# A new order of the same units, with eight products on another engine

## The chip, the cores and the metric

The kernel runs on one core of a Trainium2 chip. A core has five engines that work side by side, each on its own queue of instructions: TensorE (PE) multiplies matrices from SBUF into PSUM, and its weight loads (PEld) are a stream beside the matmuls; VectorE (DVE) and ScalarE (ACT) work element by element and read PSUM as well as SBUF; GpSimd (POOL) works element by element on SBUF; SyncE (SP) issues all the transfers of this kernel. Engines wait for each other through semaphores. The metric is the device time of one execution in microseconds (us); less is better.

## The reference

Two independent parts share S = 2048 positions and D = 576 channels, and their results stand side by side in the output.

```python
# part A: a short convolution, a gate, a long convolution, a gate
for t in range(ks):                                   # ks = 4
    k_shift = k_shift + k_pad[:, t:t + S, :] * shift_k[:, ks - 1 - t][None, None, :]
kv = k_shift * v
y = irfft2(rfft2(kv_pad) * rfft2(kf_pad))[:, 0, :S, :]    # length 2*S
a = q * (y + kv * ssm_D)
# part B: linear attention, 32 heads of 18
q, k, v = split(x @ wqkv)
phi = lambda t: jnp.where(t > 0, t + 1, jnp.exp(t)) + 1e-6
kv = einsum("bhsd,bhse->bhde", phi(k), v);  z = einsum("bhsd->bhd", phi(k))
o = einsum("bhqd,bhde->bhqe", phi(q), kv) / (einsum("bhqd,bhd->bhq", phi(q), z)[..., None] + 1e-6)
b = o.reshape(B, S, D) @ wo
```

All data is bf16. `ssm_k` has one filter of 2048 taps for each channel.

## The kernel before

The work is cut into 333 units, each a small function. `ORDER` is a text that names every unit once, in the order in which they are emitted; each engine gets its instructions in that order and runs them in that order. After the `@` of a unit stand the PSUM banks that it uses (eight banks of 512 f32), and letters before it say which engine copies the result out of PSUM: A for ACT, D for DVE. So the order of `ORDER` sets, on every engine and on SP's queue, who stands behind whom; semaphores do the rest.

Part A takes the 576 channels in five chunks (128, 128, 64, 128, 128). `h` is the filter, `u` the gated input. For each chunk: `hl` loads the filter, `hd` adds ssm_D to its first tap (ACT), `hT` transposes it on PE. `cv` is the short convolution, in four stages: a product of k with the broadcast weights Wj into `at` (L495, L497), a sum (L498), and at the end the gate with v (L501). The long convolution is a Fourier transform in two steps: `h1`, `u1` multiply with the tables G (L530), and their results Ch and Cu are transposed by DMA (`ht`, `ut`, L538) into Cth and Ctu, `h2`, `u2` multiply with a small table W (L554) into T and SU. `pX` and `pT` are the products of the two spectra (L565, L567). `i1` and `j1` are the first step back (L580, with V as the result), `i2` the second, with the tables F, and the gate with q (L601, L602, L608). `sv` and `st` store. The tables G come from `ix` (the index, L146 to L153) and `sin` (L218); the second table takes the absolute value of the index, `mc`, computed on DVE (L153).

Part B: `q`, `kt` and `k` are the projections (L477, L471, L453, L462), each followed by phi: an exponential on ACT (L447) and a minimum and maximum on DVE (L448) that reads the result in SBUF and the projection in PSUM. `Gt` and `G` multiply phi(k) with x (L651, L663); `kv`, `M`, `z`, `ez`, `den`, `bc` are the small matrices and the normalisation (`bc` is L744 and L750 for the wide part, L755 and L758 for the rest); `o` and `ot` the output (L771, L774, L785, L788), stored by `os`.

At the start `wu` issues 40 matmuls on zeros (L80) that wait for one memset of DVE. `wm` writes a row of ones and zeros into the weights wq and wk (L366, L367), so that the bias-like extra row of x is handled by the same matmul; `lw` loads wq and wk. `xl` loads x, `xT` and `xU` transpose two of its four parts on PE and `xd` two by DMA. POOL makes index tables and masks (`hc`: L89 to L115) and clears rows. `fz` and `wx` are places for filler matmuls; with the letter N they emit nothing.

Two helpers matter. `evict` (L298 to L302) copies PSUM to SBUF on ACT or DVE. `in_turn` (L396) is called in front of a product: where it runs on POOL, DVE first clears one element and POOL copies that element, so that POOL's product can't begin before DVE has come to this place in its own queue. In the kernel before no unit has the letter P, so nothing of this is emitted.

Of the kernel before, what the change touches and what calls it, by code (L numbers as in the profile page):

```python
# [27 lines left out]


ORDER = """  # L30
wm hl.0 io wu.0 wx.5.N@0 wx.3.N@1 wx.2.N@2 wu.40@3 ix.0 hd.0 iw wx.1.N@0 sin.1 xl.1 wk id wx.4.N@0 ix.1 hT.0.A@4
xU.1.D@0 xT.1.D@6 ls Wj.0.A@2 wx.0.N@0 Wj.1.A@0 xl.3 one h1.0.0.1.D@4 iv xU.3.D@6 xT.3.D@2 h1.0.1.1.D@0 sin.0 sw
W lw.0 q.1.0@4 q.1.4@5 q.1.2@6 lw.1 kt.1@2 k.6@0 k.4@1 eps k.7@3 kl.0 cv.0.0. q.3.4@2 cv.0.1. h1.0.0.0.A@4
kt.3@0 hl.1 cv.0.2. h1.0.1.0.A@6 hd.1 k.5@1 q.1.1@3 q.1.3@2 q.3.3@4 q.3.2@0 hT.1.A@6 vl.0 hl.2 k.13@5 k.14@1
k.15@2 hd.2 q.3.0@3 cv.0.3. ht.0.0 h2.0.0.0.A@6 h2.0.0.1.A@4 k.12@0 q.3.1@1 hc h1.1.1.1.A@2 xd.2 q.2.4@4 k.9@5
h1.1.1.0.A@6 k.8@2 kt.2@0 cv.1.0. cv.1.1. hl.4 hd.4 h1.1.0.0.A@6 k.11@1 h1.1.0.1.A@4 ht.0.1 fz.7.N@0
h2.0.1.0.A@2 h2.0.1.1.A@6 q.2.1@0 q.2.3@4 k.10@2 cv.1.2. u1.0.1.0.A@6 xd.0 k.3@1 q.0.4@0 u1.0.0.0.A@4 kt.0@2
q.0.0@3 xl.2 u1.0.1.1.A@6 k.0@4 cv.1.3. u1.0.0.1.A@0 q.0.3@2 ht.1.0 h2.1.0.1.A@6 h2.1.0.0.A@4 k.1@0 cv.2.0. xl.0
k.2@1 ht.1.1 h2.1.1.0.A@6 h2.1.1.1.A@4 cv.2.1. cv.2.2. FT.0 Gt@3 u1.1.0.0.A@6 fz.4.N@0 u1.1.0.1.A@4 fz.6.N@0
u1.1.1.1.A@0 q.0.1@2 cv.2.3. G.4@6 ut.0.0 u2.0.0.0.A@4 ut.0.1 u2.0.1.0.D@0 q.2.0@2 u1.2.0.1.A@6 fz.3.N@3  # L40
u1.1.1.0.A@4 z@3 hT.2.D@0 u2.0.1.1.A@6 ez@2 den.3@3 den.1@4 u2.0.0.1.A@0 Wj.2.A@2 pX.0.0. pT.0.0. u1.2.1.0.A@6
FT.1 G.3@5 kl.1 u1.2.0.0.A@0 bc.1.0@26 q.0.2@4 u1.2.1.1.A@0 q.2.2@5 ut.1.1 u2.1.1.1.A@2 u2.1.1.0.A@6 ut.1.0
pX.0.1. ut.2.0 h1.2.1.1.A@0 ql.0 G.2@4 h1.2.1.0.A@2 hl.3 vl.1 pT.0.1. cv.3.0. cv.3.1. i1.0.1@60 den.0@5
j1.0.1.AA@60 h1.2.0.0.A@2 G.0@4 u2.1.0.1.A@6 i1.0.0@02 pX.1.1. pT.1.1. u2.1.0.0.A@4 j1.0.0.AA@02 cv.3.2. G.1@6
pX.1.0. pT.1.0. bc.0.0@40 h1.2.0.1.A@2 lwv hd.3 i2.0.0.A@6 i2.0.1.A@2 hT.3.A@4 cv.3.3. ht.2.0 i1.1.1@60
j1.1.1.AA@60 h1.3.0.1.A@2 kv@4 h1.3.0.0.A@6 h1.3.1.0.D@0 h1.3.1.1.A@2 u2.2.0.0.A@4 u2.2.0.1.D@6 h2.2.0.0.D@0
h2.2.0.1.A@2 den.2@4 lwo M.4@6 M.2@2 M.3@0 pX.2.0. i1.1.0@64 bc.1.4@2 bc.2.4@0 j1.1.0.AD@64 M.1@2 bc.0.4@0
ht.3.0 h2.3.0.1.D@6 pT.2.0. h2.3.0.0.A@4 i2.1.1.A@2 M.0@0 ht.3.1 u1.3.1.0.A@6 u1.3.0.1.D@4 u1.3.1.1.A@2 hT.4.D@0
u1.3.0.0.A@6 ut.3.1 cv.4.0. i2.1.0.A@4 h2.3.1.0.A@2 i1.2.0@06 h2.3.1.1.A@4 cv.4.1. cv.4.2. j1.2.0.AA@06 o.0.AA@2
ot.0.A@4 i2.2.0.A@0 i2.2.1.A@6 fz.9.F@2 u2.3.1.0.A@4 bc.2.0@20 h1.4.0.0.A@6 h1.4.1.1.A@4 h1.4.1.0.A@2  # L50
h1.4.0.1.A@6 u2.3.1.1.A@0 ot.2.A@4 fz.8.N@2 cv.4.3. o.2.DA@2 ut.3.0 u2.3.0.0.A@6 u2.3.0.1.D@0 pX.3.0. st
ot.1.A@4 u1.4.1.1.A@2 ht.4.1 pT.3.0. ht.4.0 u1.4.0.1.A@6 u1.4.0.0.A@4 os.0 o.3.DA@0 u1.4.1.0.A@2 os.7 i1.3.0@64
os.6 h2.4.1.0.A@0 pX.3.1. j1.3.0.AA@64 os.2 h2.4.1.1.D@2 pT.3.1. ut.4.0 o.1.AD@0 h2.4.0.1.D@2 h2.4.0.0.A@6
i1.3.1@40 bc.3.4@6 j1.3.1.AA@40 bc.3.0@26 ut.4.1 ql.1 u2.4.0.0.A@4 u2.4.0.1.A@2 pX.4.0. os.5 o.4.AD@0 pT.4.0.
fz.0.N@2 ot.3.A@4 o.5.DA@6 os.4 os.9 u2.4.1.1.A@2 i1.4.0@40 u2.4.1.0.D@6 pX.4.1. os.8 pT.4.1. j1.4.0.AA@40
o.6.AA@2 os.12 os.1 os.3 os.14 i2.3.1@6 sv.3.1 os.10 i2.3.0@4 sv.3.0 fz.2.N@0 i1.4.1@02 j1.4.1.DA@02 o.7.DA@6
os.15 os.13 os.11 i2.4.0@4 sv.4.0 i2.4.1@2 sv.4.1 fz.5.N@0 fz.1.F@0
"""


# [78 lines left out]
def _dft_index(tc, slot, K, part):  # L139

    nc = tc.nc
    if part == 0:
# [4 lines left out]

        nc.vector.tensor_scalar(out=K.mp[:], in0=K.mp[:], scalar1=19, scalar2=19, op0=ALU.logical_shift_left,
                                op1=ALU.arith_shift_right)
# [91 lines left out]
def kernel(  # L241
# [121 lines left out]
    def one_w():  # L363

        for w in (wk, wq):
            nc.vector.memset(w[0:64, 4, :].bitcast(I32), 0)  # L366
# [519 lines left out]
```

## Time and profile before

| what | value |
|---|---|
| time, median of 3 runs | 173.18 us (170.98 to 174.4) |
| time of the profiled execution | 170.53 us |
| its span, first to last instruction | 168.8 us |
| granted TensorE clock, mean | 0.99 |
| busiest engine | PE, 91% of the span |
| data moved | 31.83 MB, mean 189 GB/s |

The profile of an execution lists how long each engine was busy, cuts the span into slices, groups instructions by their line in the kernel (L530 is line 530), and says for each idle stretch which other instruction ended it ("<-"). "issue" is time in which an engine waited for nothing that the profile shows. x16 behind a group is the number of its instructions. SPq is SP's queue; for a transfer, its row there is the time that SP took to issue it, and "to landing" the time from issue until the data is there. Busy times of PE are modelled from pipelined matmuls and overlap.

### The profile page before, as it was taken

How to read it: one execution, taken by the hardware profiler on the slowest of the kernel's cores; microseconds unless marked ns; L12 is line 12 of the kernel's file. 1: busy time of each engine (PE TensorE's matmuls, PEld its weight loads, DVE VectorE, ACT ScalarE, POOL GpSimd, SP SyncE). 2: the span in 40 equal slices, each digit the busy share in tenths (PEclk: the TensorE clock that was granted, in tenths of full speed). 3: DMA queues.
4: the chain of work that ended last, by engine and by line, in shares of the span. 5: the costliest groups of instructions: out<-in, count | busy, mean ns of one | idle time of the engine just before them, and what ended most of it. 6: DMA issues, size and time to landing. Idle time of an engine off the chain costs nothing.

```text
span 168.8 us, 6523 instructions
## 1 busy us (share of the span) xinstructions
PE 153.5 (91%) x2899; PEld 96.9 (57%) x2920; DVE 146.8 (87%) x183; ACT 130.7 (77%) x172; POOL 22.3 (13%) x57
## 2 busy tenths in 40 slices
...
GB/s 131 293 317 267 337 252 155 233 161 203 152 220 193 179 140 132 267 184 53 204 346 260 82 215 156 128 128 6 123 147 296 159 196 169 165 276 83 201 240 91
DMA packets 74464, 31.83 MB, mean 189 GB/s; under 512 B 52361, under 2 KB 73859, under 8 KB 74436
## 3 DMA queue, kind: packets, MB, share of 16 engines
...
q8 instruction: 22, 0.36, 0.9%
...
HBM read 14.90 MB, written 4.72 MB: 116 GB/s over the span
## 4 chain that ended last, share of the span: by engine, by line
PE 75%; DVE 9%; ACT 8%; issue 3%; DVEq 1%
PE banks L663 10%; PE banks L530 9%; PE banks L453 9%; PE banks L477 8%; PE banks L771 7%; PE banks L580 5%; PE banks L554 5%; ACT V L300 3%; PE banks L517 3%; PE banks L80 3%; ACT T L300 2%; PE banks L601 2%; PE banks L602 2%; DVE at L498 2%; PE banks L651 2%
## 5 line engine op out<-in xcount | busy, mean ns | idle before, releaser
L300 ACT ACTIVATE V<-banks 128x1024 bf16<-128x1024 f32 (+1 forms) x22 | 21.4, 1026 | 5.6 <-PE banks L580 5.0
L530 PEld LDWEIGHTS <-G 128*128 128x128 bf16 x320 | 17.8, 98 | 5.8 <-issue 2.5
L453 PE MATMUL banks<-wk,xT 128*128 128x512 bf16 x73 | 18.7, 379 | 0.5 <-issue 0.2
L477 PE MATMUL banks<-xT,wq 128*128 128x512 bf16 x77 | 18.8, 380 | 0.2
L300 ACT ACTIVATE Cu<-banks 128x1024 bf16<-128x1024 f32 (+1 forms) x19 | 17.0, 940 | 1.2 <-ACT T L300 1.0
L498 DVE TENSOR_TENSOR at<-at 128x2048 bf16<-128x2048 bf16 (+1 forms) x15 | 17.5, 1164 | 0.5
L663 PE MATMUL banks<-pk,x_sb 128*128 128x512 bf16 (+1 forms) x77 | 17.6, 379 | 0.2
L497 DVE TENSOR_TENSOR at<-k,Wj 128x2048 bf16<-128x2048 bf16 (+1 forms) x15 | 17.0, 1131 | 0.1
L300 ACT ACTIVATE Ch<-banks 128x1024 bf16<-128x1024 f32 (+1 forms) x17 | 15.2, 928 | 1.3 <-PE banks L530 1.1
L771 PE MATMUL banks<-late_w,pqT 128*128 128x512 bf16 x57 | 14.8, 380 | 0.6 <-ACT T L300 0.2
L300 ACT ACTIVATE SU<-banks 128x1024 bf16<-128x1024 f32 x14 | 14.2, 1029 | 0.6 <-PE banks L554 0.5
L300 ACT ACTIVATE T<-banks 128x1024 bf16<-128x1024 f32 x14 | 13.9, 1039 | 0.2 <-PE banks L554 0.2
L448 DVE SCALAR_TENSOR_TENSOR pk<-pk,banks 128x512 bf16<-128x512 bf16 (+1 forms) x20 | 12.3, 630 | 1.5 <-ACT pk L447 1.4
L447 ACT ACTIVATE pk<-banks,neg 128x512 bf16<-128x512 f32 (+1 forms) x20 | 12.6, 656 | 1.2 <-PE banks L453 1.1
L447 ACT ACTIVATE pqT<-banks,neg 128x512 bf16<-128x512 f32 x16 | 11.0, 693 | 2.6 <-PE banks L477 2.2
L663 PEld LDWEIGHTS <-x_sb 128*128 128x128 bf16 (+1 forms) x80 | 7.7, 100 | 8.4
L580 PE MATMUL banks<-W,X 32*128 32x64 bf16 x576 | 11.2, 190 | 1.4 <-issue 1.4
L565 DVE TENSOR_TENSOR X<-SU,T 128x2048 bf16<-128x2048 bf16 x9 | 10.8, 1202 | 1.8 <-ACT SU L300 1.2
L530 PE MATMUL banks<-hT,G 128*128 128x128 bf16 (+1 forms) x160 | 11.1, 214 | 1.2 <-ACT Ch L300 0.9
L453 PEld LDWEIGHTS <-xT 128*128 128x128 bf16 x80 | 7.2, 98 | 8.5 <-issue 1.6
L477 PEld LDWEIGHTS <-wq 128*128 128x128 bf16 x80 | 7.2, 98 | 8.4 <-issue 1.0
L448 DVE SCALAR_TENSOR_TENSOR pqT<-pqT,banks 128x512 bf16<-128x512 bf16 x16 | 10.6, 682 | 1.5 <-ACT pqT L447 1.4
(146 smaller groups left out, 312.9 us busy)
## 6 DMA issues: line engine op xcount, KB each, us to landing
...
```

The lines of the kernel that those rows point to most:

```text
L300: nc.scalar.activation(out=out, in_=in_, func=ACT.Copy)
L447: nc.scalar.activation(out=out_ap, in_=ps_ap, func=ACT.Exp, bias=K.neg1[0:n, :])
L448: nc.vector.scalar_tensor_tensor(out=out_ap, in0=out_ap, scalar=1.0, in1=ps_ap, op0=ALU.min, op1=ALU.max)
L453: nc.tensor.matmul(ps, lhsT=xT[r // 4][:, t, r % 4 * 128:(r % 4 + 1) * 128], rhs=wk[:, t, 0:512], start=(t == 0), stop=(t == 4))
L477: nc.tensor.matmul(ps, lhsT=wq[:, t, 128 * c:128 * c + 128], rhs=xT[g][:, t, :], start=(t == 0), stop=(t == 4))
L497: in_turn(on[0]).tensor_tensor(out=t_, in0=kk[:, 3 - stage:19 - stage], in1=wb(stage), op=ALU.mult)
L498: in_turn(on[1]).tensor_tensor(out=a_, in0=a_, in1=t_, op=ALU.add)
L530: nc.tensor.matmul(ps[:, bi, 0:dc].rearrange("p (z h y) -> p z h y", z=2, y=8), lhsT=K.G[ri][:, b, :], rhs=xf(b).rearrange("p (h z y) -> p ...
L565: in_turn(on).tensor_tensor(out=s['X', hf][:], in0=s['SU', hf][:], in1=t[:, :, ::-1, :], op=ALU.mult)
L580: nc.tensor.matmul(ps[r][:, j, z, g, :], lhsT=s[key, hf][q:q + 32, z, x, 128 * g:128 * g + 128], rhs=K.W[q:q + 32, m, :], start=(n == 0), ...
L663: nc.tensor.matmul(ps[0:fn, :], lhsT=x_sb[:, r, f0:f0 + fn], rhs=pk[:, r, 0:512], start=(r == 0), stop=(r == 15))
L771: nc.tensor.matmul(ps[:, hh, :], lhsT=pqT[:, 4 * g + 2 * hh + i, c, :], rhs=B['M'][:, c, 0:512], start=(c == 0), stop=False)
```

## The change

`ORDER` is replaced by another order of the same 333 units, with other banks and other letters for the copies. Eight products now carry the letter P and run on POOL: the sum of stage 2 and the first product of chunk 1 in the short convolution (`cv.0.2.DP`, `cv.1.0.P`), and of the spectra `pX.1.0`, `pT.2.0`, `pX.3.1`, `pT.3.0`, `pT.4.1`, `pT.4.0`. The rows of `wm` are written by POOL, and the absolute value of the index is taken by ACT. The remaining lines of the kernel stay; all line numbers after `ORDER` grow by one. At the start of SP's queue the order of loads was h, x, shift weights, x, wq, wk, k, h; it becomes h, shift weights, x, x, h, wq, wk, k, and three transposes of Ch now follow before the first DMA transpose of x, where it was one.

```diff
 ORDER = """
-wm hl.0 io wu.0 wx.5.N@0 wx.3.N@1 wx.2.N@2 wu.40@3 ix.0 hd.0 iw wx.1.N@0 sin.1 xl.1 wk id wx.4.N@0 ix.1 hT.0.A@4
-xU.1.D@0 xT.1.D@6 ls Wj.0.A@2 wx.0.N@0 Wj.1.A@0 xl.3 one h1.0.0.1.D@4 iv xU.3.D@6 xT.3.D@2 h1.0.1.1.D@0 sin.0 sw
-W lw.0 q.1.0@4 q.1.4@5 q.1.2@6 lw.1 kt.1@2 k.6@0 k.4@1 eps k.7@3 kl.0 cv.0.0. q.3.4@2 cv.0.1. h1.0.0.0.A@4
...
-os.15 os.13 os.11 i2.4.0@4 sv.4.0 i2.4.1@2 sv.4.1 fz.5.N@0 fz.1.F@0
+io wu.0 wk wx.5.N@0 wu.40@1 wx.4.N@0 ix.0 sin.1 id iw hl.0 hd.0 ls Wj.0.D@2 Wj.1.D@4 hT.0.D@6 iv wx.2.N@0 ix.1
+sin.0 fz.8.N@1 wx.3.N@2 xl.1 xT.1.D@4 h1.0.1.1.A@6 xU.1.A@0 h1.0.1.0.A@2 xl.3 hl.1 one xU.3.D@1 h1.0.0.1.D@4
+hd.1 h1.0.0.0.A@6 eps xT.3.D@0 hT.1.D@2 wx.1.N@4 lw.0 sw wm q.1.4@4 q.3.1@0 lw.1 k.13@1 W q.3.0@2 h1.1.0.1.A@6
+wx.0.N@0 k.15@0 kl.0 ht.0.1 vl.0 kt.3@1 h1.1.1.1.A@4 h1.1.1.0.A@6 cv.0.0.D cv.0.1.DD cv.0.2.DP h1.1.0.0.A@2
+k.12@0 h2.0.1.0.A@4 h2.0.1.1.A@6 q.3.2@1 fz.2.N@2 q.1.0@3 k.14@4 q.3.4@5 k.7@6 q.3.3@0 cv.0.3.DDD cv.1.0.P k.6@1
+q.1.2@3 ht.1.0 h2.1.0.0.A@4 h2.1.0.1.A@6 q.1.3@0 kt.1@2 q.1.1@4 ht.1.1 h2.1.1.0.A@6 k.5@5 Wj.2.A@1 k.4@3
+fz.1.F@0 h2.1.1.1.A@6 u1.0.1.0.A@0 u1.0.1.1.A@4 cv.1.1.DD fz.7.N@2 fz.5.F@2 xd.2 hl.2 cv.1.2.DD u1.0.0.1.A@6
+q.2.4@2 hd.2 k.10@0 u1.0.0.0.A@4 k.8@1 cv.1.3.DDD hT.2.A@6 k.9@3 q.2.2@2 ht.0.0 h2.0.0.0.A@4 h2.0.0.1.A@6
+q.2.1@0 xd.0 k.11@1 q.0.3@4 cv.2.0.D u1.1.0.1.A@6 k.1@5 u1.1.1.0.A@2 k.3@0 kt.2@1 cv.2.1.DD u1.1.1.1.A@6 ut.0.1
...
+cv.4.1.DD cv.4.2.DD j1.2.0.AA@64 M.0@2 hT.4.D@0 M.3@6 i2.2.0.A@4 i2.2.1.A@2 M.1@6 h1.4.0.0.A@4 bc.2.4@0
+h1.4.1.0.D@2 cv.4.3.DDD ut.3.1 u2.3.1.0.A@6 h1.4.1.1.A@0 h1.4.0.1.A@4 u2.3.1.1.A@2 pX.3.1.P o.5.DA@6 ot.3.A@0
+ut.3.0 u2.3.0.0.A@4 u2.3.0.1.A@2 st u1.4.1.0.D@0 u1.4.0.0.A@6 ot.2.D@4 u1.4.1.1.A@2 ht.4.1 u1.4.0.1.A@0
+bc.1.0@46 h2.4.1.0.A@2 h2.4.1.1.A@0 pT.3.1.D o.6.AA@4 ht.4.0 pX.3.0.D pT.3.0.P i1.3.1@62 bc.1.4@0 j1.3.1.DA@62
+h2.4.0.1.D@4 o.4.AD@0 os.11 h2.4.0.0.A@2 ut.4.1 bc.0.4@6 u2.4.1.0.A@4 ut.4.0 os.10 i1.3.0@06 os.9 u2.4.1.1.D@2
+pX.4.1.D pT.4.1.P j1.3.0.AA@06 o.2.DA@4 ot.1.D@2 os.6 bc.0.0@06 ql.1 o.3.DD@4 u2.4.0.0.A@2 u2.4.0.1.A@0 pX.4.0.D
+pT.4.0.P o.7.AA@6 os.15 os.7 os.5 os.12 i1.4.1@24 j1.4.1.AA@24 os.14 ot.0.A@0 i2.3.1@6 sv.3.1 o.0.AA@2 os.0 os.8
+i2.3.0@4 sv.3.0 os.2 os.13 i1.4.0@06 j1.4.0.AD@06 os.4 fz.6.N@2 o.1.AD@2 os.3 os.1 i2.4.1@4 sv.4.1 fz.0.N@0
+i2.4.0@0 sv.4.0
 """
@@ _dft_index
-        nc.vector.scalar_tensor_tensor(out=K.mc[:], in0=K.mp[:], scalar=-1.0, in1=K.mp[:], op0=ALU.mult, op1=ALU.max)
+        nc.scalar.activation(out=K.mc[:], in_=K.mp[:], func=ACT.Abs)
@@ one_w
-            nc.vector.memset(w[0:64, 4, :].bitcast(I32), 0)
-            nc.vector.memset(w[0:1, 4, :].bitcast(I32), 0x3F803F80)
+            nc.gpsimd.memset(w[0:64, 4, :].bitcast(I32), 0)
+            nc.gpsimd.memset(w[0:1, 4, :].bitcast(I32), 0x3F803F80)
```

More of the change, by code (lines that the diff above doesn't have):

```diff
@@ L30 @@
 ORDER = """
-wm hl.0 io wu.0 wx.5.N@0 wx.3.N@1 wx.2.N@2 wu.40@3 ix.0 hd.0 iw wx.1.N@0 sin.1 xl.1 wk id wx.4.N@0 ix.1 hT.0.A@4
-xU.1.D@0 xT.1.D@6 ls Wj.0.A@2 wx.0.N@0 Wj.1.A@0 xl.3 one h1.0.0.1.D@4 iv xU.3.D@6 xT.3.D@2 h1.0.1.1.D@0 sin.0 sw
-W lw.0 q.1.0@4 q.1.4@5 q.1.2@6 lw.1 kt.1@2 k.6@0 k.4@1 eps k.7@3 kl.0 cv.0.0. q.3.4@2 cv.0.1. h1.0.0.0.A@4
-kt.3@0 hl.1 cv.0.2. h1.0.1.0.A@6 hd.1 k.5@1 q.1.1@3 q.1.3@2 q.3.3@4 q.3.2@0 hT.1.A@6 vl.0 hl.2 k.13@5 k.14@1
-k.15@2 hd.2 q.3.0@3 cv.0.3. ht.0.0 h2.0.0.0.A@6 h2.0.0.1.A@4 k.12@0 q.3.1@1 hc h1.1.1.1.A@2 xd.2 q.2.4@4 k.9@5
@@ L36 @@
[L36 to L55, printed above, removed]
@@ L56 @@
-o.6.AA@2 os.12 os.1 os.3 os.14 i2.3.1@6 sv.3.1 os.10 i2.3.0@4 sv.3.0 fz.2.N@0 i1.4.1@02 j1.4.1.DA@02 o.7.DA@6
-os.15 os.13 os.11 i2.4.0@4 sv.4.0 i2.4.1@2 sv.4.1 fz.5.N@0 fz.1.F@0
+io wu.0 wk wx.5.N@0 wu.40@1 wx.4.N@0 ix.0 sin.1 id iw hl.0 hd.0 ls Wj.0.D@2 Wj.1.D@4 hT.0.D@6 iv wx.2.N@0 ix.1
+sin.0 fz.8.N@1 wx.3.N@2 xl.1 xT.1.D@4 h1.0.1.1.A@6 xU.1.A@0 h1.0.1.0.A@2 xl.3 hl.1 one xU.3.D@1 h1.0.0.1.D@4
+hd.1 h1.0.0.0.A@6 eps xT.3.D@0 hT.1.D@2 wx.1.N@4 lw.0 sw wm q.1.4@4 q.3.1@0 lw.1 k.13@1 W q.3.0@2 h1.1.0.1.A@6
@@ new lines @@
+q.2.1@0 xd.0 k.11@1 q.0.3@4 cv.2.0.D u1.1.0.1.A@6 k.1@5 u1.1.1.0.A@2 k.3@0 kt.2@1 cv.2.1.DD u1.1.1.1.A@6 ut.0.1
+u1.1.0.0.A@2 q.2.0@4 kt.0@0 u2.0.1.0.D@6 u2.0.1.1.A@2 xl.0 q.2.3@1 ut.0.0 h1.2.1.0.A@4 k.2@0 h1.2.1.1.A@2
+u2.0.0.1.A@6 xl.2 pX.0.1.D pT.0.1.D u2.0.0.0.A@4 k.0@1 hl.3 hd.3 h1.2.0.1.A@2 Gt@0 h1.2.0.0.A@6 ut.1.1
+u2.1.1.0.A@4 pX.0.0.D pT.0.0.D u2.1.1.1.A@2 G.4@1 ut.1.0 u2.1.0.1.A@6 FT.1 cv.2.2.DD cv.2.3.DDD i1.0.1@42
+u2.1.0.0.A@0 j1.0.1.AD@42 q.0.4@6 q.0.2@7 hc z@0 ht.2.0 kl.1 u1.2.1.1.A@4 hT.3.D@2 h2.2.0.0.A@6 ez@0 den.3@1
@@ new lines @@
+u1.2.0.1.A@4 u1.2.1.0.A@2 pX.1.0.P u1.2.0.0.A@6 q.0.1@0 bc.3.0@42 G.1@1 i1.0.0@64 FT.0 h2.2.0.1.A@2 pT.1.0.D
+ut.2.0 j1.0.0.AD@64 den.2@0 q.0.0@1 h1.3.1.0.A@2 h1.3.1.1.A@4 h1.3.0.0.A@6 G.0@0 h1.3.0.1.A@2 pX.1.1.D pT.1.1.D
+cv.3.0.D cv.3.1.DD ql.0 i2.0.0.A@4 i2.0.1.A@6 i1.1.1@02 u2.2.0.1.A@4 j1.1.1.AA@02 G.2@6 u2.2.0.0.A@4 i1.1.0@02
+j1.1.0.AA@02 vl.1 cv.3.2.DD cv.3.3.DDD pX.2.0.D fz.9.N@6 ht.3.0 h2.3.0.1.A@6 hl.4 hd.4 cv.4.0.D fz.4.N@4
+fz.3.N@4 G.3@5 pT.2.0.P bc.3.4@0 bc.2.0@26 ht.3.1 den.1@4 u1.3.0.0.A@0 den.0@5 u1.3.0.1.A@2 i2.1.1.A@0
```

1 line of the change is left out of this document (added).

## The prediction

> **What bounds the kernel now.** I read the page first: how full each engine is over the span.
>
> ```profile
> span 168.8 us, 6523 instructions
> PE 153.5 (91%) x2899; PEld 96.9 (57%) x2920; DVE 146.8 (87%) x183; ACT 130.7 (77%) x172; POOL 22.3 (13%) x57
> ```
>
> PE is idle for 168.8 - 153.5 = 15.3 us. Both orders hold the same 333 units, so its matmuls stay, and those 15.3 us are all that can be won. The view of stretches says where they lie (span, PE, PEld, DVE, ACT, POOL, clock, DMA share, GB/s).
>
> ```profile
> 2.50:20.00 17.50, 17.32 (x171) 12.86 (x175) 16.11 (x28) 12.98 (x17) 9.80 (x27) 1.00 1.05 297
> 20.00:40.00 20.00, 19.65 (x175) 10.91 (x177) 19.33 (x25) 17.39 (x26) 8.43 (x10) 1.00 1.02 209
> 40.00:60.00 20.00, 19.84 (x277) 11.98 (x277) 18.59 (x25) 19.03 (x28) 0.52 (x1) 1.00 0.93 187
> 60.00:80.00 20.00, 19.84 (x270) 11.25 (x270) 16.69 (x26) 14.37 (x22) 0.73 (x1) 1.00 0.87 154
> 80.00:100.00 20.00, 18.26 (x481) 11.39 (x482) 18.17 (x17) 14.89 (x20) 1.21 (x2) 1.00 0.92 217
> 100.00:120.00 20.00, 18.28 (x580) 14.07 (x581) 18.98 (x22) 18.12 (x23) 0.00 (x0) 1.00 0.65 116
> 120.00:140.00 20.00, 18.58 (x379) 11.68 (x382) 17.73 (x18) 18.71 (x26) 0.00 (x0) 1.00 0.96 192
> 140.00:161.80 21.80, 20.54 (x571) 12.07 (x572) 17.62 (x19) 13.77 (x18) 0.00 (x0) 1.00 0.79 179
> 161.80:168.80 7.00, 1.20 (x16) 0.71 (x13) 2.27 (x2) 0.00 (x0) 0.00 (x0) 0.77 0.66 156
> ```
>
> Of these 5.8 us lie after 161.8 (7.00 - 1.20), where the last products and stores run and where both orders end alike. From 2.5 to 80 PE is idle for 0.85 us, from 80 to 161.8 for 6.1. So the first half can only be harmed, and the second can give at most 6.1. The waits of PE name the causes, and the 2.5 us before the first matmul.
>
> ```profile
> PE banks L80 <- DVE sm L82: 2.5, 1, 2.5
> PE banks L580 <- issue: 1.4, 2, 1.1
> PE banks L554 <- ACT V L300: 1.4, 3, 0.8
> PE banks L530 <- ACT Ch L300: 0.9, 2, 0.6
> PE banks L728 <- ACT SU L300: 0.5, 1, 0.5
> ```
>
> What PE waits for in the second half is evictions by ACT (2.8 us in these rows), busy for 36.8 of the 40 us from 100 to 140, and 1.4 us of "issue".
>
> **The start: a gain that I give back.** The change takes four bias memsets from the head of DVE's queue and moves the absolute value from DVE to ACT.
>
> ```profile
> 0.92 0.30 DVE L366 MEMSET wk<- 64x288 int32 x1 [0.92 <-PEq L870]
> 2.30 0.06 DVE L128 MEMSET negpi<- 128x1 f32 x1
> 2.52 4.45 PE L80 MATMUL banks<-sm 128*128 128x128 bf16 x40 [2.52 <-DVE sm L82]
> 6.04 1.92 ACT L218 ACTIVATE G<-mp 128x2048 bf16<-128x2048 int32 x1 [0.25 <-DVE mp L148]
> 13.02 1.24 PE L477 MATMUL banks<-xT,wq 128*128 128x512 bf16 x4
> wk<-in_B_wqkv_dram SPq DMA_DIRECT2D x1, 72.0 KB, 9.0
> 5.21 1.51 SPq L374 DMA_DIRECT2D wk<-in_B_wqkv_dram  x1
> 10.86 0.55 PE banks L530 x8
> 35.00 1.08 PE banks L477 x5
> 115.14 1.04 PE banks L517 x16
> ```
>
> DVE's first constant comes 2.30 - 0.92 = 1.38 us earlier, and so do the warm matmuls: 1.15 to 5.6. Then ACT is late next. Its chain is a sine (from 6.04 - 1.38 = 4.7), a short bias step (I count 0.3), the absolute value and the other sine; both have the first sine's shape, so 1.9 each. That ends at 4.7 + 1.9 + 0.3 + 1.9 + 1.9 = 10.7, and ACT's first eviction follows. PE needs that eviction's bank for its fourth product with G, and ACT's third for the second transpose of h, which I place near 14 to 15. The first projection stands behind it: at 15.0 instead of 13.02. But PE has by then done two more products with G (0.55 each) and one more transpose of h (1.04), 2.1 us of work, against 2.0 us of delay. Net nothing. I take 0, between -1.4 (nothing given back) and +1.5 (below).
>
> On SP's queue one more load of h, 512 KB, now stands ahead of the weights. wk came at 5.21 + 9.0 = 14.2. 524 KB at the 297 GB/s of that stretch are 1.8 us, so wk comes at 16.0; PE asks for it after a short projection of q (some 0.7) and a full one (1.08), at 16.8. Cover 0.8 us; 1 us later, and PE pays 0.2 and whatever follows. Adding PE's units on from there, the first transposed tile is asked for near 23.5, not at 33.3, and stands behind k on the same queue:
>
> ```profile
> 33.26 0.56 PE banks L554 x16
> 23.59 3.23 SPq L538 DMA_TRANSPOSE Cth<-Ch  x1
> Cth<-Ch SPq DMA_TRANSPOSE x1, 5.9
> 9.44 5.39 SPq L440 DMA_DIRECT2D h_sb<-in_A_ssm_k_dram  x1
> ```
>
> SP was free of as many bytes (all up to that load of h) at 9.44 + 5.39 = 14.8. A transpose issued at 15 lands 5.9 later, at 21: cover 2.5 us. The next two follow v and are issued 3.2 us apart, with about 3 us each. So no loss is counted, though none of these covers is thick.
>
> **Eight products on POOL.** POOL does six of the products of the spectra and two steps of the first convolutions. Here are the rows for DVE's price, and for POOL beside DVE.
>
> ```profile
> L567 DVE TENSOR_TENSOR T<-SU,T 128x2048 bf16<-128x2048 bf16 x9 | 11.0, 1222 | 0.2
> L448 DVE SCALAR_TENSOR_TENSOR pk<-pk,banks 128x512 bf16<-128x512 bf16 x16 | 10.8, 684 | 1.5 <-ACT pk L447 1.4
> L750 DVE SCALAR_TENSOR_TENSOR pqT<-pqT,banks 128x1024 bf16<-128x1024 bf16 x8 | 9.4, 1218 | 2.5 <-PE banks L744 2.5
> 20.94 0.66 POOL L110 TENSOR_SCALAR_AFFINE_SELECT esel<-esel 32x576 bf16<-32x576 bf16 x1
> 23.27 1.53 POOL L110 TENSOR_SCALAR_AFFINE_SELECT esel<-esel 32x576 bf16<-32x576 bf16 x1
> 24.32 1.57 DVE L498 TENSOR_TENSOR at<-at 128x2048 bf16<-128x2048 bf16 x1
> ```
>
> DVE sheds 8 x 1.22 = 9.8 us. No product runs on POOL in this trace. A select of 576 elements with one input takes 0.66 us there, 1.15 ns an element: 2.3 us for 2048, and 4.7 when two inputs are read in turn. Beside DVE's sums of two SBUF tensors the same select takes 1.53, at worst thus 2 x 1.53/576 x 2048 = 10.9 us. I take 4.7, since each product is put where DVE reads PSUM: in the order of the instructions a small memset on DVE releases POOL, and the DVE work behind it is phi steps, normalisations and evictions. Until the first DVE instruction that needs the product that is: six phi of 0.684 and a short one, 4.5 us (first); 5.8; 0.68 + 2 x 1.22 = 3.1 (third, X of chunk 1); the other five have 4.7 us and more, or their reader is PE, 8 us on. So DVE stands 0.2 us at the first and 1.6 at the third. Queued behind that wait is one half of an eviction of V, whose bank PE wants later. I count +0.3. Behind POOL's own waits stand the row of ones of xT, masks and two clearings, with several us to spare.
>
> [...]
>
> **80 to 161.8.** Five or six of the eight products lie here: DVE falls from 72.5 us (the four stretches) to about 66. But PE waits for ACT, whose total hardly changes: copies of hT and Wj leave it, evictions of T and SU and the absolute value come. Adding up both orders with these durations, ACT has done some 2.5 us more by the PE work that ends at 80, and has that much less behind it; that is what can shorten its 36.8 us of 40, and PE feels it only where ACT is last. DVE's lead also frees banks earlier. Of the 6.1 us I let a quarter go: -1.5. The ends are 0 and -4.7, the 6.1 less the 1.4 of "issue".
>
> **Sum.** 0 + 0.3 - 1.5 = -1.2 us. The profiled execution took 170.53 us, its span of 168.8 and 1.7 around it; after it would be 169.3, a factor of 0.993. It was faster than all three timed runs (median 173.18, 170.98 to 174.4), so in the median I expect 0.993 x 173.18 = 172.0. Runs of one program lie 2% apart, so 2% either way, 3.5 us, is what a measurement can tell from no change.
>
> **Rivals.** *Faster* (0.28). The start's 1.4 us are kept and DVE's freedom ends the ACT waits: -1.4 - 4.7 = -6.1, 164.4, in the median 167.0. For it: DVE is at 18 to 19 of 20 us in four stretches, and everything in them leans on it. Against it: the rows name ACT, not DVE.
>
> *Slower* (0.17): instruction fetch.
>
> ```profile
> 89.45 0.23 PE L580 MATMUL banks<-W,X 32*128 32x64 bf16 x5 [0.32 <-issue]
> 100.02 0.23 PE L580 MATMUL banks<-W,X 32*128 32x64 bf16 x6 [1.10 <-issue]
> 157.38 1.15 PE banks L580 x128
> q8 instruction: 22, 0.36, 0.9%
> ```
>
> The inverse transform (L580) has 128 matmuls and 128 weight loads in 1.2 us, and PE stopped twice inside it for its own instructions. There are nine such pairs. Moved, each may meet a fetch behind transfers: five pairs at 1.1 are 5.5 - 1.4 = +4.1, 174.6, in the median 177.3; from five it decides, nine would be +8.5. For it: the DMA share is 0.65 to 0.96 here. Against it: seven of nine pass untouched now, and several halves are now set apart by a product with x. [...]
>
> *Slower, early* (0.08): a cover of the start fails, the first transpose or wk coming 3 us late, +3 to +5 us, 175 in the median and above. *About the same* (0.47): the forecast.
>
> **How the numbers follow.** The forecast's own bounds are -1.4 more (the start kept) and +1.5 over no gain: 167.9 to 172.0 in the profile, 170.5 to 174.7 in the median. Faster by over 2% is the first rival and 0.01 of the forecast's edge, 0.29; slower by over 2% the two others, 0.25; the rest is 0.46. The range takes in the first rival's 167.0 and the fetch rival at five pairs, 177.3.
>
> **What the next profile should show.** Warm matmuls from about 1.2 us; the first projection near 15; wk just in time; POOL's products at 4 to 5 us with no sum of two SBUF tensors on DVE beside them; DVE near 136 us, PE as before; PE's idle time in 2.5 to 80 under 2 us, and after 80 around 4.5. I am wrong if a product takes 6 us or more and DVE stands behind it, if PE waits for a transposed tile (L554's successor) or a weight before 40 us, or if "issue" inside the inverse transforms passes 4 us.

## The result and the profile after

The changed kernel takes 168.77 us in the median of four runs (168.21 to 170.11), the kernel before 172.11 (four runs, 170.98 to 174.4). The ratio is **0.986, with a 95% interval of 0.981 to 0.991**: about 2.4 us less, a gain, but less than the 2% that I had named as the least to be told. A second session gave 0.9865 (0.982 to 0.991). The forecast was 0.993, with 172.0 us and a range from 167.0 to 177.3. The ratios here and below leave out executions in a slower state, over 1.5% above the fastest of the same kernel or at a lower clock (one of 504 us in a later run is among them), so they are not the quotients of the medians beside them.

The profiled execution took 170.11 us, the slowest of the four; its span is 168.1 us. From its page, the busy times:

```profile
PE 156.1 (93%) x2899; PEld 98.6 (59%) x2920; DVE 137.5 (82%) x180; ACT 128.2 (76%) x171; POOL 58.6 (35%) x77
```

DVE is down by 9.3 us, POOL up by 36.3. PE is busy for 2.6 us more with the same 2899 matmuls, so some of them ran slower. The stretches (columns as in the prediction: span, PE, PEld, DVE, ACT, POOL, clock, DMA share, GB/s):

```profile
2.50:20.00 17.50, 17.26 (x161) 13.94 (x160) 13.38 (x21) 12.90 (x15) 7.54 (x27) 1.00 1.00 279
...
80.00:100.00 20.00, 18.20 (x419) 11.17 (x420) 15.91 (x18) 13.27 (x18) 4.24 (x2) 1.00 0.91 198
100.00:120.00 20.00, 19.51 (x500) 13.09 (x499) 18.84 (x21) 17.20 (x22) 5.45 (x4) 1.00 0.78 152
120.00:140.00 20.00, 18.66 (x388) 11.53 (x389) 17.68 (x22) 17.27 (x24) 7.45 (x4) 1.00 0.82 174
140.00:161.80 21.80, 20.94 (x575) 12.44 (x576) 13.53 (x18) 12.72 (x17) 9.52 (x5) 1.00 0.69 180
```

PE's idle time from 80 to 161.8 is 1.80 + 0.49 + 1.34 + 0.86 = 4.5 us, where it was 6.1. Most of the 1.80 is one stop, and it heads the waits of PE (in total, times, longest):

```profile
PE banks L664 <- issue: 1.7, 1, 1.7
...
PE banks L555 <- ACT Cu L301: 0.9, 2, 0.5
PE banks L581 <- POOL T L568: 0.6, 1, 0.6
```

At the start the matmuls tell why PE is busier. PE's timeline after the change, and then a transpose of x of the same shape before (start, duration):

```profile
1.18 4.45 PE L81 MATMUL banks<-sm 128*128 128x128 bf16 x40 [1.18 <-DVE sm L83]
...
9.33 1.91 PE L338 MATMUL banks<-ident,x_sb 128*128 128x128 bf16 x16
...
14.42 1.06 PE L338 MATMUL banks<-ident,x_sb 128*128 128x128 bf16 x16
...
16.41 0.74 PE L472 MATMUL banks<-xT,wq 128*64 128x256 bf16 x10
```

```profile
8.84 1.06 PE L337 MATMUL banks<-ident,x_sb 128*128 128x128 bf16 x16
```

Sixteen transposes of x take 1.91 us at 9.33 and 1.06 at 14.42: PE runs at about half rate until some 13.5 us. Before, it had its full rate at 8.84. The warm matmuls (those on zeros) began 1.3 us earlier, and PE stayed slow until some 5 us later. The clock column shows 1.00 here all the same; only the durations tell.

### The profile page after: what moved, and what is told of

Same layout as the page of the kernel before. It is cut to its first block, busy times and chain, and to the rows that moved or that the text cites. A ratio compares the mean times of both kernels' runs of the same rounds, so it can differ in the third digit from the quotient of the medians.

```text
span 168.1 us, 6554 instructions
## 1 busy us (share of the span) xinstructions
PE 156.1 (93%) x2899; PEld 98.6 (59%) x2920; DVE 137.5 (82%) x180; ACT 128.2 (76%) x171; POOL 58.6 (35%) x77
## 4 chain that ended last, share of the span: by engine, by line
PE 82%; issue 3%; ACT 3%; DVE 3%; POOL 3%; DMA 2%; DVEq 1%; SPq 0%; POOLq 0%
PE banks L664 11%; PE banks L454 11%; PE banks L531 11%; PE banks L478 10%; PE banks L772 6%; PE banks L581 6%; PE banks L555 6%; PE banks L518 3%; PE banks L602 3%; POOL T L568 2%; DMA Wrow<-in_A_shift_k_dram 2%; PE banks L603 2%; PE banks L786 2%; PE banks L472 2%; PE banks L338 2%
## 5 line engine op out<-in xcount | busy, mean ns | idle before, releaser
L403 POOL COPY ones<-ones 1x1 bf16<-1x1 bf16 x8 | 1.4, 178 | 71.6 <-DVE ones L402 71.6
L301 ACT ACTIVATE V<-banks 128x1024 bf16<-128x1024 f32 (+1 forms) x20 | 19.4, 1014 | 2.8 <-PE banks L581 1.8
L531 PEld LDWEIGHTS <-G 128*128 128x128 bf16 x320 | 18.4, 100 | 3.8 <-issue 0.7
L454 PE MATMUL banks<-wk,xT 128*128 128x512 bf16 x76 | 19.7, 380 | 0.2
L664 PE MATMUL banks<-pk,x_sb 128*128 128x512 bf16 (+1 forms) x78 | 18.2, 380 | 1.8 <-issue 1.7
L301 ACT ACTIVATE SU<-banks 128x1024 bf16<-128x1024 f32 x16 | 15.9, 1031 | 3.4 <-PE banks L555 3.4
L301 ACT ACTIVATE T<-banks 128x1024 bf16<-128x1024 f32 x17 | 16.9, 1031 | 1.3 <-PE banks L555 1.1
L301 ACT ACTIVATE Ch<-banks 128x1024 bf16<-128x1024 f32 (+1 forms) x18 | 16.3, 937 | 2.0 <-PE banks L531 2.0
L568 POOL TENSOR_TENSOR T<-SU,T 128x2048 bf16<-128x2048 bf16 x4 | 16.3, 4064 | 0.3
L499 DVE TENSOR_TENSOR at<-at 128x2048 bf16<-128x2048 bf16 (+1 forms) x14 | 15.9, 1135 | 0.6
L301 ACT ACTIVATE Cu<-banks 128x1024 bf16<-128x1024 f32 (+1 forms) x18 | 16.0, 934 | 0.1
L664 PEld LDWEIGHTS <-x_sb 128*128 128x128 bf16 (+1 forms) x80 | 7.6, 100 | 10.8 <-issue 2.6
L581 PE MATMUL banks<-W,T 32*128 32x64 bf16 x576 | 11.0, 192 | 0.6 <-POOL T L568 0.6
## 6 DMA issues: line engine op xcount, KB each, us to landing
k<-in_A_k_dram SPq DMA_DIRECT2D x1, 1280.0 KB, 10.4
```

The source lines that it names most:

```text
L301: nc.scalar.activation(out=out, in_=in_, func=ACT.Copy)
L454: nc.tensor.matmul(ps, lhsT=xT[r // 4][:, t, r % 4 * 128:(r % 4 + 1) * 128], rhs=wk[:, t, 0:512], start=(t == 0), stop=(t == 4))
L499: in_turn(on[1]).tensor_tensor(out=a_, in0=a_, in1=t_, op=ALU.add)
L531: nc.tensor.matmul(ps[:, bi, 0:dc].rearrange("p (z h y) -> p z h y", z=2, y=8), lhsT=K.G[ri][:, b, :], rhs=xf(b).rearrange("p (h z y) -> p ...
L568: in_turn(on).tensor_tensor(out=t[:], in0=s['SU', hf][:], in1=t[:], op=ALU.mult)
L581: nc.tensor.matmul(ps[r][:, j, z, g, :], lhsT=s[key, hf][q:q + 32, z, x, 128 * g:128 * g + 128], rhs=K.W[q:q + 32, m, :], start=(n == 0), ...
```

## The experiments

Where the gain came from was open between three explanations: the products taken off DVE, the new order with its two line edits, and the rate of PE at the start. Each experiment changes one of them or a part of it. Each was timed against the kernel before on the same chip. Of the two line edits together I speak as "the edits" (absolute value on ACT, rows of the weights on POOL), of the eight units with the letter P as "the products". These are the combinations that were run:

| order | edits | products on POOL | ratio to before | 95% interval |
|---|---|---|---|---|
| old | yes | none | 1.0135 | 1.008 to 1.019 |
| old | no | all eight | 1.149 | 1.142 to 1.157 |
| old | no | six of the spectra | 1.080 | 1.072 to 1.087 |
| new | no | none | 1.038 | 1.029 to 1.046 |
| new | no | all eight | 1.011 | 1.005 to 1.018 |
| new | yes | none | 1.0043 | 1.0005 to 1.008 |
| new | yes | two of the convolution | 0.9991 | 0.996 to 1.002 |
| new | yes | six of the spectra | 0.989 | 0.985 to 0.993 |
| new | yes | all eight | 0.986 | 0.981 to 0.991 |

### The products taken back

```diff
-cv.0.2.DP  cv.1.0.P  pX.1.0.P  pT.2.0.P  pX.3.1.P  pT.3.0.P  pT.4.1.P  pT.4.0.P
+cv.0.2.DD  cv.1.0.D  pX.1.0.D  pT.2.0.D  pX.3.1.D  pT.3.0.D  pT.4.1.D  pT.4.0.D
```

> The new order with its eight products put back on DVE; everything else stays. Theory A (the relief of DVE is the gain of the second half): DVE is at about 147 us again, PE's idle time between 80 and 161.8 goes back from 4.5 towards 6 us or more, and the time is 0.995 to 1.01 of the kernel before. Theory B (the order's shift of ACT work is the gain, DVE was not what PE waited for): the ratio stays at 0.986 within 0.004, since DVE had room, and PE's wait of 0.6 us for a product of POOL goes.

It took 172.03 us, 1.0043. New order and edits without the products win nothing; the products are worth 1.0043 - 0.986 = 1.8%, 3.1 us. The waits of PE for DVE that this kernel has and the changed one lacks, and the stretch with most of PE's idle time:

```profile
PE banks L531 <- DVE ob L303: 0.8, 1, 0.8
PE banks L772 <- DVE pqt L759: 0.6, 1, 0.6
PE banks L772 <- DVE ob L303: 0.6, 1, 0.6
...
120.00:140.00 20.00, 17.52 (x371) 11.23 (x374) 18.05 (x21) 16.95 (x23) 0.00 (x0) 1.00 0.79 175
```

All three end with DVE, 2.0 us together: two with copies that free a bank, one with a step of the normalisation (L759). From 80 to 161.8 the rows of ACT come to 1.3 us here (0.8 for Cu, 0.3, 0.2) and those of DVE to 2.2; in the kernel before they were 3.5 (1.4, 0.9, 0.5, 0.3, 0.2, 0.2) and 0.2. So with the new order ACT's waits did shrink, and DVE's took their place. One part of the expectation missed: PE's idle time there is 0.65 + 0.66 + 2.48 + 0.91 = 4.7 us, not 6 or more. That is 0.2 more than in the profile above, which holds the stop of 1.7 us, and 1.9 more than in the second profile of the changed kernel (below), which doesn't. Waits of 1.3 us for the first transposed tile and 0.5 for wk stand in this profile as well; they vary between executions, as shown further down.

### Which of the eight

```diff
-pX.1.0.P  pT.2.0.P  pX.3.1.P  pT.3.0.P  pT.4.1.P  pT.4.0.P
+pX.1.0.D  pT.2.0.D  pX.3.1.D  pT.3.0.D  pT.4.1.D  pT.4.0.D
```

> The changed kernel with only the two products of the short convolution on POOL; the six of the spectra go back to DVE. All eight back on DVE gave 1.0043, all eight on POOL 0.986. If each product counts alike (1.2 us less on a DVE that is the bound throughout): a quarter of the gain, 0.9997. If only the place counts where PE was seen to stand in the kernel with all eight on DVE (20 to 40 us 1.4 us more than in the changed kernel, 120 to 140 us 1.1 us more): a little over half of the gain, 0.994, with the loss in 120 to 140 us (PE 17.5 of 20) still there.

And the other half, with only the two of the convolution taken back:

```diff
-cv.0.2.DP  cv.1.0.P
+cv.0.2.DD  cv.1.0.D
```

> The changed kernel with only the six products of the spectra on POOL; the two of the short convolution go back to DVE. If each product counts alike: three quarters of the gain, 0.9906. If the place counts: a little under half, 0.995, with PE near 18.4 of 20 us in the stretch from 20 to 40 (a transposed tile that comes late) and near 18.7 from 120 to 140.

The two alone gave 0.9991, the six alone 0.989. Against 1.0043 that is 0.5% and 1.5%, a quarter and three quarters, as if each product counted alike. My other reading, that the place where PE was seen to stand decides, falls: the six alone left PE idle for 1.55 us from 20 to 40, the very stretch that I had charged to the two, and won 1.5% all the same.

```profile
20.00:40.00 20.00, 18.45 (x174) 9.07 (x176) 18.77 (x25) 17.67 (x26) 0.52 (x1) 1.00 1.07 206
```

The two alone were expected at 0.9997 or 0.994, the six at 0.9906 or 0.995. The intervals are 0.003 to 0.004 wide on either side; an equal price for each is what fits best, not more.

### The same products in the old order

```diff
-cv.0.2.  cv.1.0.  pX.1.0.  pT.2.0.  pT.3.0.  pX.3.1.  pT.4.0.  pT.4.1.
+cv.0.2.DP  cv.1.0.P  pX.1.0.P  pT.2.0.P  pT.3.0.P  pX.3.1.P  pT.4.0.P  pT.4.1.P
```

> The order before, with the same eight products on POOL and nothing else changed. Theory A (relief of DVE): faster than the kernel before by 0.5 to 1.5%. Theory B (the products need the places that the new order gives them): 1.00 to 1.02, because DVE's next two-input instructions on SBUF stand right behind the products here and either wait for them or run slower beside them; POOL's products then take more than the 4.06 us that they take in the new order.

198.78 us, 1.149: 26 us more than before, far beyond both expectations. The waits of PE:

```profile
PE banks L580 <- POOL T L567: 7.8, 3, 2.7
PE banks L471 <- POOL xT L355: 7.1, 1, 7.1
```

Two things show. First, the inverse transform (L580) stands close behind the products of the spectra in the old order and waits for POOL's slower ones (4.07 us in the row below, where DVE took 1.22). Second, PE waits 7.1 us for a row of xT that POOL clears in 0.51. POOL's timeline shows why:

```profile
26.69 0.18 POOL L402 COPY ones<-ones 1x1 bf16<-1x1 bf16 x1 [11.49 <-DVE ones L401]
26.95 4.07 POOL L498 TENSOR_TENSOR at<-at 128x2048 bf16<-128x2048 bf16 x1
...
42.92 0.51 POOL L355 MEMSET xT<- 1x512 bf16 x1
```

POOL stands 11.49 us in `in_turn` until DVE comes to that place, and then does its product and nearly 12 us of masks before the row. To separate the two I took the convolution's products away and kept the six:

```diff
-cv.0.2.DP  cv.1.0.P
+cv.0.2.  cv.1.0.
```

> The order before with only the six spectrum products on POOL; the two of the short convolution stay on DVE. If the 1.149 of all eight came from the place of the two in POOL's queue (a row of xT behind them: 7.1 us of PE, and DVE and ACT late behind that): the wait for xT goes, 15 to 20 us less, 1.04 (the waits for T in the inverse transforms, 7.8 us, stay). If it came from the readers of the spectra standing close behind them: 1.10 or more.

186.06 us, 1.080. The wait for xT is gone, and with it some 12 us; I had expected 15 to 20. The rest stays, and more of it than I had summed: three waits for T, and one of 3.1 us for a copy by DVE.

```profile
PE banks L580 <- POOL T L567: 7.5, 3, 2.7
PE banks L601 <- DVE Cu L302: 3.1, 1, 3.1
```

The second row is POOL's work too. These are POOL's product and DVE's step beside it in this run, and then the same step before:

```profile
113.56 4.08 POOL L567 TENSOR_TENSOR T<-SU,T 128x2048 bf16<-128x2048 bf16 x1
114.09 4.09 DVE L608 TENSOR_TENSOR q<-V,q 128x1024 bf16<-128x1024 bf16 x1 [0.92 <-ACT V L300]
```

```profile
114.47 0.68 DVE L608 TENSOR_TENSOR q<-V,q 128x1024 bf16<-128x1024 bf16 x1
```

The gate (L608) reads two tensors in SBUF, takes 4.09 us instead of 0.68, and ends 0.54 us after the product. The copy of Cu stands behind it in DVE's queue. PE's rate suffers as well, as in the last stretch:

```profile
140.00:161.80 21.80, 15.63 (x458) 8.37 (x457) 10.14 (x13) 12.31 (x15) 11.09 (x5) 0.92 0.79 160
```

The granted clock is 0.92 there, where the kernel before had 1.00. Right behind the wait of 3.1 us, from 119.3 to 122.4, it is 0.51, and 1.00 again from 122.4 to 126: in this run a PE that stood for some us was also slowed afterwards. So the six products that win 1.5% in the new order cost 8% in the old one. What the new order gives them, as far as these rows show, is room between a product and its reader, and no DVE step on two SBUF tensors beside it. The two orders differ in banks and copy letters too, which were not tried apart.

### The edits alone, and undone

In the old order, the edits alone:

```diff
-        nc.vector.scalar_tensor_tensor(out=K.mc[:], in0=K.mp[:], scalar=-1.0, in1=K.mp[:], op0=ALU.mult, op1=ALU.max)
+        nc.scalar.activation(out=K.mc[:], in_=K.mp[:], func=ACT.Abs)
...
-            nc.vector.memset(w[0:64, 4, :].bitcast(I32), 0)
-            nc.vector.memset(w[0:1, 4, :].bitcast(I32), 0x3F803F80)
+            nc.gpsimd.memset(w[0:64, 4, :].bitcast(I32), 0)
+            nc.gpsimd.memset(w[0:1, 4, :].bitcast(I32), 0x3F803F80)
```

> The order before, with only the two small edits: bias rows by POOL, absolute value by ACT. My prediction (the start's 1.4 us are given back to ACT's chain): 1.00 within 0.004, the first warm matmul at 1.2 us and the first projection at 13 as before or a little later. Rival (the early start is kept): 0.992. Second rival (the bias rows stand late in POOL's queue, and ACT's copy of hT waits behind the absolute value): 1.005 to 1.01.

174.17 us, 1.0135, above all three expectations. There they cost. PE begins 1.3 us earlier and then stands for the identity matrix of DVE; its first projection starts at 14.00 us instead of 13.02. From PE's timeline, its three longest waits after the start:

```profile
7.16 1.86 PE L517 MATMUL banks<-ident,h_sb 128*128 128x128 bf16 x16 [1.54 <-DVE ident L69]
...
105.91 0.61 PE L530 MATMUL banks<-hT,G 128*128 128x128 bf16 x8 [1.60 <-ACT Ch L300]
...
147.81 0.63 PE L554 MATMUL banks<-Ctu,W 64*32 64x512 bf16 x16 [1.85 <-DMA Ctu<-Cu]
```

Until 80 us PE is 0.8 to 1.0 us behind the same matmuls of the kernel before, at the end 2.3. So under half of the loss comes at the start; the rest comes after 100 us, and how the edits lead to those two waits isn't shown.

Then the changed kernel with that same diff reversed (absolute value on DVE, rows by DVE; order and products as changed):

> The changed kernel with the two code edits undone: absolute value on DVE, rows of the weights by DVE; order and POOL products stay. My forecast's step (start: net nothing): 0.986, ACT's chain ending 1.9 us earlier and nothing gained by it. Rival, the edits cost here too, as they did in the old order (1.0135 there): 0.973. Rival, DVE has no room for them before 20 us: 0.995 or more, PE under 16.5 of 17.5 us in the stretch from 2.5 to 20.

174.45 us, 1.011, as in the last of the three expectations: without the edits the new order loses 2.5%, more than all it wins. PE's waits at the head of its list, and the two instructions of DVE behind them:

```profile
PE banks L531 <- ACT G L219: 2.9, 1, 2.9
PE banks L472 <- DVE wq L368: 2.4, 1, 2.4
```

```profile
10.15 2.28 DVE L154 SCALAR_TENSOR_TENSOR mc<-mp 128x2048 int16<-128x2048 int32 x1
...
22.23 0.30 DVE L368 MEMSET wq<- 1x288 int32 x1
```

The absolute value, ready to run at 5, stands behind the copies of Wj and hT in DVE's queue until 10.15, and with it ACT's second sine and the table G: 2.9 us of PE. The last row of wq is written at 22.23, behind copies that follow PE; the first projection has begun at 19.57, and its last two matmuls, which need that row, start at 22.59: 2.4 us. Both are 0.3 to 2.3 us of work on DVE, dear by their place in its queue. Last, both kinds of help taken away, the order alone (the two diffs above reversed together):

> The new order alone: absolute value and weight rows on DVE, all eight products on DVE. If the two parts act apart (edits 1.011 against 0.9865, products 1.0043 against 0.986): 1.011 + 0.018 = 1.029, PE standing for G (2.9 us) and for wq (2.4) before 25 us and for transposed tiles, bank copies by DVE later. Rival, the early delay gives DVE's later work room, so that the products cost nothing more: 1.011 to 1.015.

178.63 us, 1.038 (1.029 to 1.046); 1.029 was expected if the two parts act apart. With no edits the products are worth 1.038 - 1.011 = 2.7%, with them 1.8%, a difference within the intervals. The rival, that the early delay gives DVE room and the products could then be left out for nothing, is refuted.

### A faster start

```diff
-wu.40@1
+wu.64@1
```

> The new kernel with 64 matmuls on zeros at the start instead of 40. In the profile of the new kernel PE ran its first work at half rate until 13.4 us (16 transposes of x in 1.71 us, against 0.89 in the kernel before, where full rate came at 8.6). Theory C (this slow start costs the new kernel 1 to 3 us, and a longer run of matmuls brings full rate earlier): full rate by 10.3 us at the latest, the ratio to the kernel before 0.970 to 0.982. Rival (ACT's chain sets the start, PE's rate there costs nothing): 0.986 within 0.004, or up to 0.99 because the first real matmuls come 1 us later.

170.53 us, 0.9926 (0.989 to 0.996): 0.7% behind the changed kernel, and just above the 0.99 at which the rival ended. What it loses is not shown. The timeline of PE shows x transposed in 1.05 us instead of 1.91, and where the gain goes:

```profile
9.91 1.05 PE L338 MATMUL banks<-ident,x_sb 128*128 128x128 bf16 x16 [0.87 <-DVE Wj L303]
...
25.28 0.62 PE L555 MATMUL banks<-Cth,W 64*32 64x512 bf16 x16 [1.18 <-DMA Cth<-Ch]
```

PE comes to the first transposed tile sooner, and waits for it: it starts there at 25.28, against 24.95 in the profile of the result. The 24 more matmuls are not needed for the full rate. The run with two products of the convolution has 40 of them, and the same instructions on PE up to there:

```profile
8.97 1.05 PE L338 MATMUL banks<-ident,x_sb 128*128 128x128 bf16 x16 [0.71 <-DVE Wj L303]
...
25.30 0.63 PE L555 MATMUL banks<-Cth,W 64*32 64x512 bf16 x16 [2.13 <-DMA Cth<-Ch]
```

In the runs with the edits and these 40, the first full rate comes between 5.1 us (the run with six products, where the clock falls back to half from 8.5 to 11.9) and 13.6 (the second profile of the changed kernel), so it varies between executions. In six profiles, the run with 64 among them, the first projection starts anywhere from 14.56 to 16.60 us, and the products with the first transposed tile from 24.95 to 26.34; the profile with the earliest tile has the second latest projection (16.41). So by these profiles the half rate at the start costs busy time, and hardly any time at the end.

### The changed kernel again, and the wait for the tile moved

> The changed kernel as it is, beside the next three on one chip. All theories: 0.986 of the kernel before, within 0.981 to 0.991.

169.25 us, 0.9865, as expected. This second profile of the same program, of a span of 167.3 us, has in its stretches from 80 on, and at the first transposed tile:

```profile
80.00:100.00 20.00, 19.84 (x446) 12.23 (x445) 17.24 (x19) 15.19 (x21) 4.24 (x2) 1.00 1.08 226
100.00:120.00 20.00, 19.36 (x513) 13.27 (x513) 18.90 (x22) 17.42 (x23) 5.46 (x4) 1.00 0.81 152
120.00:140.00 20.00, 18.74 (x386) 11.16 (x385) 17.78 (x22) 17.31 (x24) 8.15 (x4) 1.00 0.88 174
140.00:161.80 21.80, 21.06 (x574) 13.00 (x578) 13.76 (x17) 12.05 (x16) 8.83 (x5) 1.00 0.72 191
```

```profile
26.34 0.63 PE L555 MATMUL banks<-Cth,W 64*32 64x512 bf16 x16 [1.13 <-DMA Cth<-Ch]
```

The stop of 1.7 us at L664 isn't there: one program meets it in one execution and not in another. Its place is not chance, though. In the 14 profiles of this case PE stops 12 times for over 0.35 us for its own instructions ("issue"), in either order, and each time after 1,105 or 1,106, after 1,233, or after 1,360 or 1,361 matmuls, counted from the first. The stop of 1.10 us in the kernel before came after 1,360. The stop at L664 is there in three other runs (1.57, 0.64 and 1.50 us), after 1,233; with 24 more warm matmuls ahead, the one after 1,233 stands at another line (0.53 us at L531). So the place goes by the count of instructions, not by the unit that stands there, and the length, from nothing to 1.7 us, by the execution. The tile, though, is late in this profile. To move PE's work in front of it:

```diff
-k.12@0 h2.0.1.0.A@4 h2.0.1.1.A@6 q.3.2@1 fz.2.N@2 q.1.0@3 k.14@4
+k.12@0 q.3.2@1 q.1.0@3 h2.0.1.0.A@4 h2.0.1.1.A@6 fz.2.N@2 k.14@4
```

> The changed kernel with one edit in the order: two projections of q moved ahead of the first products with W, which wait for the first transposed tile. In one profile of the changed kernel PE stands there for 1.1 us, in another 0. If that wait sets the end: 0.980 (1.1 us less). If PE or a later reader catches up: 0.986.

169.68 us, 0.989 (0.983 to 0.996): nothing won. Its rows of waits, of the slowest of its six executions, show none for Cth, and a new one in its place, for the bank that the delayed eviction of T frees; the next run has the same row:

```profile
PE banks L454 <- ACT T L301: 1.1, 1, 1.1
```

### Three more products

On top of the last edit:

```diff
-pT.0.1.D  pT.0.0.D  cv.4.0.D
+pT.0.1.P  pT.0.0.P  cv.4.0.P
```

> The kernel of the run before, with three more products on POOL (two of the spectra of chunk 0, the first of the last short convolution), 3.7 us less on DVE. If DVE still holds PE back: 0.6% less than the run before (at the 0.23% that each of the eight was worth). If PE, over 98% busy in most stretches, is the bound now: the same, within 0.3%.

187.21 us, 1.0925: neither 0.6% less nor the same, 10% more than the run before. Its waits of PE:

```profile
PE banks L694 <- POOL onesr L116: 5.7, 1, 5.7
PE banks L472 <- ACT SU L301: 3.8, 1, 3.8
PE banks L675 <- POOL late_w L638: 2.1, 1, 2.1
```

L116 (the last of the masks) and L638 (a row) are small things that POOL makes behind its products: 7.8 us in a queue that has become long, as with xT above. The 3.8 us are ACT's, whose copy of SU waits until POOL's product has read the buffer (ACT's timeline):

```profile
76.62 1.94 ACT L301 ACTIVATE SU<-banks 128x1024 bf16<-128x1024 f32 x2 [3.96 <-POOL T L568]
```

So the three together found nothing to win on PE, and much to hold up; one at a time they were not tried. Beside that, POOL's products and DVE's at that time (the timelines of the two engines) show a price that I had not counted:

```profile
65.97 4.06 POOL L568 TENSOR_TENSOR T<-SU,T 128x2048 bf16<-128x2048 bf16 x1
...
72.07 4.51 POOL L568 TENSOR_TENSOR T<-SU,T 128x2048 bf16<-128x2048 bf16 x1
```

```profile
68.47 2.65 DVE L566 TENSOR_TENSOR X<-SU,T 128x2048 bf16<-128x2048 bf16 x1
...
71.99 0.69 DVE L499 TENSOR_TENSOR at<-at 128x1024 bf16<-128x1024 bf16 x1
72.71 4.42 DVE L498 TENSOR_TENSOR at<-k,Wj 128x1024 bf16<-128x1024 bf16 x1
```

DVE's step of 0.69 us, begun 0.64 after POOL's product, takes 4.42: it ends at 77.13, 0.55 after that product (72.07 + 4.51 = 76.58). The other, begun 2.50 after a product that ends at 70.03, takes 2.65 instead of the 1.22 of its shape, and ends 1.09 after it. Both end about their own usual duration after POOL's product, as if they had started when POOL was done, and so does the gate in the old order (4.09 us, ended 0.54 after).

## Why the prediction was right, and where it wasn't

The sign and the size were inside what I gave; the sum of 0 + 0.3 - 1.5 was half of the measured 2.4 us, and its one large term was put down to the wrong engine. That the number fits although the reason doesn't is luck.

**The start, net nothing.** By busy time it holds: PE is busy for 17.26 us from 2.5 to 20, where it had 17.32, though at half rate it does less in that time. The warm matmuls begin at 1.18, as foreseen. The chain of ACT held as well: its second sine ends at 10.8 (forecast 10.7). The working misses two things. The first projection came at 16.41, not at 15.0, because PE stayed at half rate till 13.5 us, which no term had; with the full rate from some 6 us on, in the run with two products, it came at 14.56. The full rate came some 12 us after the first matmul in the changed kernel, and 4 us after it at the earliest in the runs with the same start (13.5 and 5.1 less 1.18); what sets the point, no run shows. And "net nothing" is the sum of two large parts: the new order without the edits would have lost 2.5% there. I had reckoned order and edits together, so that this cost no accuracy; it was luck that I never had to price one without the other.

**The covers of the loads.** wk did come in time in the profile after; in the run without the products, where PE was earlier, PE waited 0.5 us for it. The cover of 2.5 us at the first transposed tile wasn't there: its transpose was issued at 15.7 and 15.9 us in the two profiles, a little after the 15 of the forecast, but it landed 8.5 and 10.4 us later, not 5.9. This is the mis-sized term. It costs 0 in one profile and 1.1 us in the other, less than the 3 to 5 of my early rival; putting other work in front of it won nothing. By the prediction's own signs a wait for a transposed tile before 40 us meant being wrong; in the second profile there is one.

**Products, 4.7 us each.** All eight take 4.06 to 4.07 us in the profile after:

```profile
29.03 4.06 POOL L499 TENSOR_TENSOR at<-at 128x2048 bf16<-128x2048 bf16 x1
...
152.68 4.06 POOL L568 TENSOR_TENSOR T<-SU,T 128x2048 bf16<-128x2048 bf16 x1
```

PE stands for one of them for 0.6 us and DVE for one for 0.5, against my 0.2 and 1.6 on DVE and +0.3 in the sum. DVE's 137.5 us are near the 136 forecast.

**A product beside DVE.** My worst case was a product that DVE's sums of two SBUF tensors slow down to 10.9 us, as I took the select's 1.53 us to show. That reading was wrong. Where a product met such a DVE step, in the run with three more products and in the old order, the product took 4.06 to 4.51 us, and it was the step that grew: it ended 0.54 to 1.09 us after the product. The rows of before fit this too: the sum of 1.57 us, begun at 24.32, ended at 25.89, 1.09 after the select that ran until 24.80, as if it had waited for the rest of an instruction that was nearly over. It cost the forecast nothing, since each of the eight stands where DVE reads PSUM, as I had found: beside the product at 29.03 two phi steps take 1.28 us together, no more than the 0.684 each of before.

```profile
29.34 1.28 DVE L449 SCALAR_TENSOR_TENSOR pqT<-pqT,banks 128x512 bf16<-128x512 bf16 x2
```

**80 to 161.8, -1.5.** PE's idle time there fell to 4.5 us in the profile after, as I had it, though 1.7 of it are the stop at L664, and to 2.8 in the second (20 - 19.84, and 0.64, 1.26 and 0.74 in the three stretches behind). But the reason I gave was ACT's lead, and against the faster rival I had set that "the rows name ACT, not DVE". That is the step that failed. ACT's lead came, and its rows shrank from 3.5 us to 1.3 without the products; but new order and edits alone win nothing (1.0043), since DVE's rows grew from 0.2 to 2.2 in their place. In this order, taking the products off DVE is the whole gain over the kernel before, 3.1 us for 9.8 us of DVE's work. In the kernel before ACT was the last releaser; DVE, busy for 17.7 to 19.0 of 20 us from 80 to 140, stood close behind it. The run with the products on POOL in the old order can't tell how close, since there PE waits for the products themselves.

**The rivals.** Fetch: one stop of 1.7 us in one execution, none in another, and neither inside the inverse transforms, where I had looked for it; the nine pairs never paid together, as the stops go by the count of instructions (1,105 or 1,106, 1,233, 1,360 or 1,361 matmuls). Whether a fetch stands behind them, no run shows. *Faster* had the right cause and too large a sum: the early 1.4 us were not kept, since PE at full speed waits for the tile.
